# Weights cast by the GpSimd queue in four quarters, w and u read to all partitions, one PSUM pool and a new written order, in a kernel of linear attention and a squared-ReLU MLP

## The chip, the cores and the metric

One NeuronCore of a Trainium2 chip. The metric is the device time of one execution in microseconds (us); lower is better. The kernel before takes 176.31 us, the median of three runs (175.8, 176.31, 177.17).

Engines are named as the profile names them: PE (TensorE matmuls, with its weight loads PEld), DVE (VectorE), ACT (ScalarE), POOL (GpSimd), SP (SyncE, which here only issues DMAs). A queue name with q (SPq, ACTq, POOLq) is the engine as an issuer of DMAs.

## The reference

Two parts, one after the other. First a linear attention with a decaying state, for 4 batches, 8 heads, 768 time steps and head width 48:

```python
for t in range(S):
    cur = einsum('bhd,bhe->bhde', u * k[t], v[t])
    y[t] = einsum('bhd,bhde->bhe', r[t], state + cur)
    state = w * state + einsum('bhd,bhe->bhde', k[t], v[t])
```

Its result, laid out as 3072 tokens x 384, goes through an MLP: `h = max(x @ w_in, 0)` with w_in 384 x 2048, and `out = (h * h) @ w_out` with w_out 2048 x 384. All tensors are float32; the kernel works in bf16 with float32 sums.

## The kernel before, in words

The time axis is cut into 6 chunks of 128 steps; with 4 batches that makes 24 chunk-items, numbered i = 4 * chunk + batch. A chunk-item's attention is done in closed form by matmuls, and its 128 rows of output are then 128 tokens of the MLP. Tokens are grouped: chunk-items 0 and 1 are groups 1-item wide (g = 0, 1), and from there two items make a group (g = 2 is items 2 and 3, g = 3 is 4 and 5, up to g = 12).

The order of the work is written out by hand in the text `ORDER` (lines 20 to 107) and nothing reorders it: each word is one step, `name.arguments:engine/buffers`, and every engine does its own steps in the order of the text, waiting by semaphores for data and for free buffers. The steps, with their lines:

- `ld.r.i`, `ld.k.i`, `ld.v.i` (L320, on SP): load one item of r, k or v, 128 x 384 float32, in runs of 48 numbers. Each of the three has 7 buffers.
- `w`, `u` (L274, L277), `shw`, `shu` (L283, L286): w and u come as four rows into partitions 0, 32, 64 and 96, and a DVE stream shuffle copies them to all partitions. `logw`, `Wk`, `Wt` (L289 to L301, on ACT) make decay factors of w; those for the first four items are in PSUM banks.
- `kh`, `rh` (L336, L339): k and r times decay factors, in bf16, into a buffer `rk`. `T` (L363, PE) transposes `rk` for items 0 to 8 and 11, and `Tc` copies it out of PSUM; for the other 14 items `XB` (L369) does the same as a transposing DMA on SP.
- `A` (L376, PE): the 128 x 128 scores of 8 heads; `Bm` (L384, DVE): the causal mask; `vb`: v in bf16; `Y` (L392, L394, PE): output, with the state of the chunk before; `U` (L403, PE), `ts`, `S` (L421, L424): the new state, for chunk c+1 of the same batch, so `S.i` is needed by `Y.(i+4)`.
- `P0`, `P1`, `du`, `dv` (L342 to L354): the diagonal term with u; `xs` (L411, DVE) adds it to `Y`. `X` (L429, PE) with `xTc`, or `xX` (L436, a transposing DMA), gives the transposed tokens.
- `F1.g.s` (L445, PE, 8 per two-item group, 4 per one-item group): one bank of x @ w_in, which covers 512 columns of the bank; `re` (L453 on ACT, L455 on DVE) the ReLU; `sq` the square, in form 0 on ACT (L460), form 1 on DVE from the bank and the ReLU (L462), form 2 on DVE from the ReLU alone (L464). `F2.i.q` (L472, PE): a quarter of the sum of item i over w_out. `os`, `out` (L484, L487): copy out of PSUM and store.
- `Z.n.b` (L481): n matmuls that compute nothing that is used.

The weights: w_in (W1) is in eight pieces of 256 columns. Seven of them are `lW` (L324): float32 loads on SP's queue into staging buffers, in the midst of the loads of r, k and v, and `cW` casts them to bf16 (six on ACT, one on POOL). The eighth, `W.0.2`, and the four quarters of w_out (W2), `W.1.0` to `W.1.3` (L333), are DMAs on POOL's queue that cast on the way. For three of the four quarters of w_out each partition takes pairs of neighbouring rows, 3072 bytes in one run.

PSUM's eight banks are divided: 4 for attention, 2 for `F1`, 2 for `F2`.

Of the kernel before, what the change touches and what calls it, by code (L numbers as in the profile page):

```python
# [18 lines left out]
POOLS = dict(ldr=7, ldk=7, ldv=7, ws=0, wsa=4, rk=7, P0=5, dv=5, vb=8, rkT=7, bank=4, bankH=2, bankO=2, Bm=6, xs=5, xT1=2, xT2=3, xT4=1, hr=6, hq=30, os=4, ts=2)  # L19
ORDER = """  # L20
ld.r.1:S/0 w:A ld.k.1:S/0 u:S Z.48.5:P tab:A ld.k.0:S/1 ld.k.2:S/2 shw:D ld.r.0:S/1 logw:A ld.r.2:S/2 Wt:A/0 P0.1:D/0
Wk:A/1 lW.0.6:S/0 kh.1:D/0 ld.v.1:S/0 rh.1:D shu:D ld.k.3:S/3 T.1:P/0 kh.0:D/1 Z.16.5:P P1.1:G Tc.1:A/0 kh.2:D/2
rh.0:D ld.v.3:S/1 WtS:A rh.2:D P0.2:G/1 A.1:P/1/2 WkS:A T.0:P/3 lW.0.1:S/1 Z.16.5:P P1.2:D ld.r.3:S/3 Tc.0:A/1
du.1:D/0 P0.0:D/2 cW.0.6:A ld.v.0:S/2 A.0:P/0/3 dv.1:G Bm.1.1:D/0 Z.6.5:P du.2:D/1 T.2:P/2 P1.0:G Bm.1.0:D/1
ld.v.2:S/3 Z.22.5:P Tc.2:A/2 Bm.0.0:D/2 Bm.0.1:D/3 lW.0.0:S/2 vb.1:A/0 lW.0.5:S/3 kh.3:D/3 Y.1:P/1 cW.0.1:A lW.0.7:S/0
A.2:P/0/2 xs.1:D/0 Z.4.5:P P0.3:G/3 vb.3:A/1 du.0:D/2 lW.0.4:S/1 X.1:P/3 Z.8.5:P rh.3:D wc:S xTc.1:A/0 Bm.2.0:D/4
vb.0:A/2 T.3:P/1 ld.k.4:S/4 dv.0:D Y.0:P/3 Z.13.5:P Tc.3:A/3 vb.2:G/3 Bm.2.1:D/5 P1.3:G xs.0:D/1 A.3:P/0/2 X.0:P/1
cW.0.0:A U.0:P/3 dv.2:G Bm.3.0:D/1 Z.6.7:P xTc.0:A/1 du.3:D/3 lW.0.3:S/2 F1.1.0:P/0 Bm.3.1:D/0 ld.r.4:S/4 F1.0.0:P/1
re.1.0:D/0 cW.0.7:G Y.2:P/0 Y.3:P/1 re.0.0:A/1 ld.k.5:S/5 xs.2:D/2 cW.0.5:A W.1.0:G dv.3:D F1.1.3:P/0 cW.0.4:A W.0.2:G
X.2:P/2 F1.0.3:P/1 re.1.3:D/2 ld.r.5:S/5 xTc.2:A/0 W.1.1:G U.2:P/0 xs.3:D/3 F1.0.2:P/0 re.0.3:A/3 sq.1.3:D2/0 WLcol:A  # L30
X.3:P/2 F1.1.2:P/1 re.0.2:D/4 xTc.3:A WLm:G U.3:P/1 F1.2.1:P/0 re.1.2:A/5 W.1.2:G sq.0.3:A0/1 F1.2.5:P/1 re.2.1:D/2
W.1.3:G sq.0.0:A0/2 U.1:P/2 S0.2:D re.2.5:A/3 F1.2.4:P/0 sq.0.2:D2/3 cW.0.3:A S0.0:D F1.2.7:P/1 re.2.4:D/1 sq.1.0:A0/4
F2.0.0:P/1 sq.2.5:D2/5 re.2.7:A/4 S0.3:D F1.0.1:P/0 F1.2.3:P/1 re.0.1:D/0 F2.1.0:P/0 S0.1:D re.2.3:A/3 F1.1.1:P/0
sq.1.2:D2/6 sq.0.1:D2/7 ld.k.7:S/6 F1.2.0:P/1 re.1.1:A/5 F2.0.1:P re.2.0:A/0 sq.1.1:D2/8 F1.2.2:P/0 sq.2.4:A0/9
sq.2.0:D1/10 F2.1.1:P kh.4:D/4 F1.2.6:P/1 ld.v.5:S/4 rh.4:D P0.4:D/4 F2.1.2:P ld.r.7:S/6 re.2.2:D/5 P1.4:G F2.0.2:P
re.2.6:D/1 sq.2.2:A0/11 F2.1.3:P ld.v.4:S/5 kh.5:G/5 sq.2.1:A0/12 sq.2.6:D1/13 F2.0.3:P os.1:A/0 du.4:D/4 ld.k.6:S/0
T.4:P/0 sq.2.3:A0/14 rh.5:D F2.2.0:P/0 os.0:A/1 P0.5:D/0 Tc.4:A/4 ld.r.6:S/0 T.5:P/3 P1.5:D F2.2.1:P kh.7:D/6 Tc.5:A/5
ld.v.7:S/6 A.4:P/1/2 du.5:D/0 F2.3.0:P/1 Bm.4.0:D/3 ld.k.9:S/2 A.5:P/0/3 vb.4:A/4 dv.4:G Bm.4.1:D/2 F2.3.1:P vb.5:A/5
ld.r.9:S/2 Bm.5.1:D/4 dv.5:G sq.2.7:A0/15 Y.4:P/1 Bm.5.0:D/5 F2.3.2:P rh.7:G ld.k.8:S/1 xs.4:D/4 U.4:P/2 Y.5:P/3
F2.2.2:P P0.6:G/1 ld.v.6:S/0 xs.5:D/0 X.4:P/0 ts.4:D/0 X.5:P/1 T.7:P/3 xTc.4:A/1 kh.6:D/1 ld.k.15:S/3 F2.2.3:P xTc.5:A  # L40
rh.6:D vb.7:A/6 U.5:P/2 P1.6:D F1.3.0:P/0 Tc.7:A/6 ld.k.10:S/4 ts.5:D/1 F1.3.1:P/1 kh.9:D/2 re.3.0:A/0 ld.v.9:S/2
T.6:P/0 P0.7:D/2 os.2:A/2 A.7:P/1/2 S.5:D re.3.1:A/5 ld.r.8:S/1 F2.3.3:P du.6:D/2 P1.7:G Tc.6:A/0 Bm.7.1:D/0
F1.3.3:P/0 sq.3.0:A0/16 rh.9:G ld.r.10:S/3 os.3:D/3 F1.3.4:P/1 re.3.3:A/2 Bm.7.0:D/1 A.6:P/3/0 P0.9:G/3 du.7:D/1
re.3.4:A/1 XB.9:S/1 F1.3.5:P/0 Bm.6.1:D/3 sq.3.1:A0/17 dv.7:G F1.3.6:P/1 Bm.6.0:D/2 re.3.5:A/3 F2.5.0:P/0 dv.6:G
vb.6:A/7 ld.k.12:S/5 sq.3.3:A0/18 Y.7:P/2 out.3:S kh.10:D/3 re.3.6:A/4 Y.6:P/1 ld.v.8:S/3 S.4:G xs.7:D/1 F1.3.2:P/0
sq.3.5:A0/19 xs.6:D/2 F1.3.7:P/1 ld.v.11:S/1 kh.8:D/0 re.3.2:A/0 kh.15:D/4 U.6:P/0 X.6:P/3 sq.3.2:A0/20 X.7:P/2 rh.8:D
F2.4.0:P/1 ld.r.12:S/4 re.3.7:A/5 rh.10:D F2.5.1:P xTc.6:A/2 sq.3.4:D2/21 P1.9:D xTc.7:A U.7:P/1 T.8:P/3 vb.9:A/2
out.0:S P0.8:D/4 F1.4.0:P/0 ts.6:D/1 ld.k.11:S/0 Tc.8:A/2 P1.8:G ts.7:D/0 F1.4.4:P/1 ld.r.13:S/5 du.9:D/3 re.4.0:A/2
F2.5.2:P kh.12:G/5 re.4.4:A/3 F1.4.6:P/0 ld.r.11:S/0 sq.3.6:A0/23 sq.3.7:D2/22 vb.8:G/3 du.8:D/4 A.9:P/2/0
sq.4.4:A0/24 A.8:P/1/3 S.6:G re.4.6:A/0 F2.5.3:P ld.v.10:S/5 Bm.8.1:D/4 F1.4.3:P/1 dv.8:G Bm.8.0:D/5 os.5:A/3  # L50
ld.k.13:S/6 F1.4.5:P/0 Bm.9.1:D/1 re.4.3:A/1 dv.9:G Y.8:P/3 Bm.9.0:D/0 re.4.5:A/5 XB.10:S/3 F2.4.1:P P0.12:G/0
xs.8:D/3 sq.4.0:A0/25 Y.9:P/1 vb.11:A/1 kh.11:G/1 F1.4.1:P/1 xs.9:D/4 ld.v.13:S/4 X.8:P/0 F1.4.2:P/0 re.4.1:D/4
xTc.8:A/0 ld.r.15:S/6 F2.4.2:P rh.11:D sq.4.1:A0/26 P1.12:D X.9:P/2 vb.10:A/0 F1.4.7:P/1 P0.10:D/1 ld.k.20:S/2 xTc.9:A
sq.4.5:D2/27 F2.7.0:P/0 P0.11:D/2 re.4.7:A/3 ld.v.12:S/6 U.8:P/3 P1.10:D sq.4.3:A0/28 F2.4.3:P kh.13:D/6 re.4.2:A/2
F1.5.2:P/1 du.10:D/0 out.1:S os.4:A/1 rh.13:G sq.4.2:A0/29 ts.8:D/1 A.10:P/1/0 ld.k.17:S/1 F2.6.0:P/1 re.5.2:A/4
P1.11:G ld.k.14:S/5 F1.5.7:P/0 rh.12:G F1.5.1:P/1 du.11:D/1 ld.k.16:S/4 re.5.7:A/5 T.11:P/2 rh.15:D re.5.1:A/1
F1.5.0:P/0 dv.10:G Bm.10.1:D/3 Tc.11:A/4 ld.v.14:S/0 F1.5.5:P/1 vb.13:D/4 re.5.0:A/2 Bm.10.0:D/2 dv.11:G U.11:P/3
A.11:P/0/2 XB.13:S/5 sq.4.7:A0/2 F2.7.1:P S.7:D re.5.5:A/3 Bm.11.1:D/4 P0.15:G/3 Y.10:P/1 sq.5.2:A0/4 F2.6.1:P
XB.12:S/6 du.12:D/2 sq.5.5:A0/7 Bm.11.0:D/5 U.9:P/2 F1.5.6:P/0 kh.17:D/0 F2.6.2:P ld.r.14:S/2 ts.9:D/0 re.5.6:A/4
Y.11:P/0 sq.5.0:D2/8 sq.5.1:A0/6 out.2:S S.9:G xs.10:D/0 F1.5.3:P/1 sq.4.6:A0/3 ld.r.16:S/1 xs.11:D/2 F1.5.4:P/0  # L60
re.5.3:D/3 S.8:G X.10:P/2 U.10:P/1 XB.15:S/0 F2.7.2:P xTc.10:A/1 P1.15:D vb.14:A/5 F2.7.3:P ts.10:D/0 dv.12:G
ts.11:D/1 ld.r.17:S/3 X.11:P/0 F2.6.3:P os.7:A/0 kh.16:D/1 xTc.11:A kh.14:D/2 A.13:P/2/1 re.5.4:A/2 ld.k.18:S/0
A.12:P/3/0 F1.6.2:P/1 sq.5.3:A0/0 sq.5.4:D2/1 S.10:D os.6:A/2 F1.6.3:P/0 re.6.2:A/1 rh.14:D ld.v.18:S/3 F2.9.0:P/0
re.6.3:A/0 rh.16:D F1.6.6:P/1 sq.5.6:A0/10 sq.5.7:D2/12 XB.14:S/2 P0.13:D/4 F2.9.1:P Bm.13.0:D/1 P1.13:G F1.6.1:P/0
Bm.13.1:D/0 XB.16:S/1 F2.8.0:P/1 P0.14:G/1 Bm.12.1:D/3 re.6.1:A/2 F2.8.1:P Bm.12.0:D/2 sq.6.3:A0/11 P1.14:G
ld.r.18:S/0 sq.6.1:A0/14 A.15:P/2/1 F1.6.4:P/0 vb.12:A/7 out.6:S Bm.15.0:D/5 P0.17:G/2 re.6.6:A/3 ld.v.17:S/2 U.13:P/0
Y.12:P/3 du.13:D/4 re.6.4:A/5 F2.8.2:P rh.17:G xs.12:D/1 ld.v.15:S/5 F1.6.0:P/1 Bm.15.1:D/4 A.14:P/2/3 du.14:D/3
re.6.0:A/4 xX.12:S/2 U.12:P/1 dv.13:D F2.8.3:P sq.6.2:A0/9 kh.18:D/3 F1.6.5:P/0 Bm.14.0:D/3 XB.17:S/3 F1.6.7:P/1
S.11:D re.6.5:A/0 ts.13:D/0 F2.9.2:P os.8:A/2 out.7:S P0.18:D/0 sq.6.0:A0/5 Y.13:P/2 ts.12:D/1 ld.k.21:S/3
sq.6.6:A0/13 F2.9.3:P P1.18:G xs.13:D/3 sq.6.5:A0/15 ld.v.16:S/1 F2.10.0:P/1 Bm.14.1:D/2 dv.14:G X.13:P/0 du.15:D/0  # L70
F2.10.1:P ld.r.20:S/4 P0.16:G/4 re.6.7:D/2 xTc.13:A Y.14:P/1 vb.15:A/6 F1.7.5:P/0 kh.20:G/6 xs.14:D/4 ld.k.22:S/6
os.9:A/0 F1.7.6:P/1 S.12:D A.16:P/2/3 xX.14:S/0 re.7.6:A/1 P1.17:G A.17:P/0/1 F2.11.0:P/0 sq.6.7:A0/16 Bm.17.1:D/1
sq.6.4:A0/17 S.13:G F1.7.1:P/1 ld.v.20:S/6 Bm.16.1:D/0 re.7.5:A/4 F2.11.1:P ld.k.19:S/5 Bm.17.0:D/2 dv.15:G Y.15:P/1
re.7.1:D/3 ld.r.19:S/6 F1.7.0:P/0 xs.15:D/0 rh.20:G F1.7.3:P/1 re.7.0:A/0 ld.r.23:S/5 P1.16:D U.15:P/3 sq.7.1:A0/20
F2.10.2:P du.16:D/1 re.7.3:A/2 U.14:P/0 xX.15:S F1.7.2:P/0 P0.20:D/1 vb.16:A/3 dv.16:G Bm.16.0:D/3 sq.7.3:A0/18
F1.7.4:P/1 out.5:S re.7.2:A/5 rh.18:D F2.11.2:P vb.18:A/1 out.8:S sq.7.6:D2/21 re.7.4:A/3 F2.10.3:P sq.7.5:D2/19
ld.r.21:S/2 kh.19:D/5 vb.17:A/2 F1.7.7:P/0 ld.k.23:S/1 sq.7.4:A0/22 rh.19:D Y.16:P/1 kh.22:D/4 re.7.7:A/2 Y.17:P/2
# [41 lines left out]
def kernel(  # L119
# [32 lines left out]

    w_in_t = moe_w_in.rearrange("(c p) f -> p c f", p=128)
    w_out_t = moe_w_out.rearrange("(q f p) o -> q p f o", f=4, p=128)
    w_out_p = moe_w_out.rearrange("(q e p j) o -> q p e j o", e=2, p=128, j=2)


    plain = {int(t.split(":")[0].split(".")[2]) // 2 for t in ORDER.split() if t.startswith("W.0.")}
# [378 lines left out]
```

## Time and profile before

The page is of one execution, whose span from the first to the last instruction is 175.6 us; the page gives no other time of it. The runs' median is 176.31 us, so 0.7 us above the span.

| | |
|---|---|
| runs | 175.8, 176.31, 177.17 us |
| span of the profiled execution | 175.6 us |
| busy: PE, DVE, ACT, POOL | 165.1, 140.6, 109.4, 69.2 us |
| first `F1` starts | 20.50 us |
| PE's last matmul ends | 172.0 us |
| granted PE clock | 1.00 throughout |
| loads of r, k, v: issue to landing, median | 4.0, 4.1, 3.8 us |
| cast DMAs of w_out: issue to landing, least, median, most | 7.4, 10.2, 11.9 us |

How to read it: a line of groups gives line, engine, operation, what it writes and reads, its count, then busy us and mean ns of one. A row of a window gives the window, its length, then each engine's busy us with the number of instructions, the PE clock, the share of the 16 DMA engines that was busy (over 1 where queues overlap) and GB/s. A row of a DMA queue gives packets, MB and the share of the 16 engines' time. "x12" is a count of instructions.

### The profile page before, as it was taken

To read this page: it belongs to the slowest core of one execution; us is meant where nothing else is said; L and a number is where in the kernel's file an instruction comes from. 1 tells how busy PE (TensorE), PEld (TensorE's weight loads), DVE (VectorE), ACT (ScalarE), POOL (GpSimd) and SP (SyncE) were. 2 spreads that over 40 slices of the span, in tenths; PEclk is the share of its full clock that TensorE was granted. 3 is DMA by queue.
4 is the path that set the end of the run, shared out by engine and by line. 5 is a ranking of instruction groups with operands and counts; after the bars stand their busy time and mean duration, and the time that the engine had idled before them with its cause. 6 is when DMAs were issued, how large, how long until landed. Compare 5 with 4: busy or idle time off the path is not lost.

```text
span 175.6 us, 4601 instructions
## 1 busy us (share of the span) xinstructions
PE 165.1 (94%) x1813; PEld 127.0 (72%) x1813; DVE 140.6 (80%) x278; ACT 109.4 (62%) x203; POOL 69.2 (39%) x84
## 2 busy tenths in 40 slices
PE   4888797899999999999999999999999999999991
PEld 4767695666778778777767787777778677787760
DVE  4699877499899998999989899899988667853620
ACT  2479498249399987886668669669478132164401
POOL 4073582035358394926282960600960302000000
PEclk9999999999999999999999999999999999999999
DMA  5999999989899999999999979989971422110041
GB/s 105 218 217 236 315 231 187 192 166 220 163 210 106 246 207 134 232 159 242 170 162 214 212 142 223 155 203 191 199 157 26 157 90 62 33 45 0 4 169 55
DMA packets 102277, 28.36 MB, mean 161 GB/s; under 512 B 94824, under 2 KB 102256, under 8 KB 102256
## 3 DMA queue, kind: packets, MB, share of 16 engines
q1 hardware_dynamic: 100360, 26.10, 75.4%
q0 software_dynamic: 1744, 1.77, 6.1%
q8 instruction: 14, 0.23, 0.6%
q10 hardware_dynamic: 152, 0.20, 0.3%
q14 instruction: 7, 0.06, 0.1%
HBM read 20.46 MB, written 4.72 MB: 143 GB/s over the span
## 4 chain that ended last, share of the span: by engine, by line
PE 80%; DMA 10%; SPq 4%; POOL 1%; issue 1%; ACT 0%; POOLq 0%
PE bank L472 36%; PE bank L445 33%; DMA wsa<-in_moe_w_in_dram 6%; DMA W<-in_moe_w_in_dram 5%; SPq L320 4%; PE bank L376 3%; PE bank L394 2%; PE bank L392 2%; PE bank L403 2%; PE bank L363 2%; PE bank L429 1%; POOL W L262 0%; SPq L324 0%; POOL W L333 0%; ACT os L260 0%
## 5 line engine op out<-in xcount | busy, mean ns | idle before, releaser
L445 PE MATMUL bank<-xT,W 128*128 128x256 bf16 (+1 forms) x624 | 74.4, 264 | 1.6 <-ACT W L260 0.9
L472 PE MATMUL bank<-W,hq 128*128 128x384 bf16 x384 | 73.6, 326 | 1.0 <-DMA W<-in_moe_w_out_dram 1.0
L453 ACT ACTIVATE hr<-bank 128x512 bf16<-128x512 f32 x71 | 42.0, 597 | 38.9 <-PE bank L445 36.3
L445 PEld LDWEIGHTS <-W 128*128 128x128 bf16 x624 | 55.3, 98 | 12.3 <-ACT W L260 1.2
L472 PEld LDWEIGHTS <-hq 128*128 128x128 bf16 x384 | 35.6, 98 | 19.0 <-issue 1.2
L460 ACT ACTIVATE hq<-hr 128x512 bf16<-128x512 bf16 x57 | 34.7, 629 | 2.5 <-DVE hr L455 2.4
L384 DVE TENSOR_TENSOR Bm<-bank,maskJT 128x512 bf16<-128x512 f32 x48 | 31.4, 683 | 3.0 <-PE bank L376 3.0
L346 POOL TENSOR_TENSOR P<-P,ub 128x384 f32<-128x384 f32 x14 | 15.2, 1086 | 35.5 <-DVE P L342 29.8
L455 DVE TENSOR_SCALAR hr<-bank 128x512 bf16<-128x512 f32 x25 | 17.1, 689 | 11.9 <-PE bank L445 8.3
L354 POOL TENSOR_TENSOR dv<-ldv,du 128x384 f32<-128x384 f32 x19 | 16.6, 886 | 23.7 <-DVE du L349 21.6
L464 DVE TENSOR_TENSOR hq<-hr 128x512 bf16<-128x512 bf16 x35 | 15.0, 457 | 1.7 <-ACT hr L453 1.7
L411 DVE TENSOR_TENSOR xs<-bank,dv 128x384 bf16<-128x384 f32 x24 | 13.2, 553 | 2.8 <-PE bank L394 2.2
L260 ACT COPY os<-bank 128x384 f32<-128x384 f32 x18 | 8.6, 477 | 8.1 <-PE bank L472 8.1
L481 PE MATMUL bank<-identity 128*128 128x128 bf16 x139 | 11.0, 242 | 2.3 <-POOL identity masks.py:199 2.3
L349 DVE TENSOR_REDUCE du<-P 128x8 f32<-128x384 f32 x24 | 12.9, 544 | 0.2 <-POOL P L346 0.2
L342 POOL TENSOR_TENSOR P<-ldr,ldk 128x384 f32<-128x384 f32 x11 | 11.3, 1024 | 2.4 <-DMA ldr<-in_r_dram 2.4
L260 ACT COPY rkT<-bank 128x1024 bf16<-128x1024 bf16 x10 | 10.1, 1015 | 2.8 <-PE bank L363 2.7
L481 PEld LDWEIGHTS <-identity 128*128 128x128 bf16 x139 | 9.7, 111 | 2.5 <-POOL identity masks.py:199 2.3
L424 POOL TENSOR_TENSOR S0W<-ts,WLm 128x384 bf16<-128x384 f32 x7 | 7.4, 1060 | 10.0 <-PE bank L472 6.7
L394 PE MATMUL bank<-vb,Bm 128*128 128x48 bf16 x192 | 10.8, 183 | 0.4 <-ACT vb L260 0.3
L394 PEld LDWEIGHTS <-Bm 128*128 128x128 bf16 x192 | 9.5, 96 | 1.4 <-issue 0.6
L260 ACT CAST vb<-ldv 128x384 bf16<-128x384 f32 x19 | 9.6, 512 | 0.0
(61 smaller groups left out, 163.8 us busy)
## 6 DMA issues: line engine op xcount, KB each, us to landing
ldr<-in_r_dram SPq DMA_DIRECT2D x24, 192.0 KB, 4.0
ldk<-in_k_dram SPq DMA_DIRECT2D x24, 192.0 KB, 4.1
ldv<-in_v_dram SPq DMA_DIRECT2D x24, 192.0 KB, 3.8
out_dram<-os SPq DMA_DIRECT2D x23, 192.0 KB, 2.1
wsa<-in_moe_w_in_dram SPq DMA_DIRECT2D x7, 384.0 KB, 4.8
W<-in_moe_w_out_dram POOLq DMA_DIRECT2D x4, 384.0 KB, 10.2
rkT<-rk SPq DMA_TRANSPOSE x14, 4.2
W<-in_moe_w_in_dram POOLq DMA_DIRECT2D x1, 192.0 KB, 8.1
```

The lines of the kernel that those rows point to most:

```text
L260: e.copy(o, a)
L346: e.tensor_mul(t, t, ub)
L354: e.tensor_mul(dvb[slot[f"dv{i}"]], loaded("v", i), t)
L384: e.tensor_mul(Bmb[slot[f"Bm{i}{h}"]], heads(bank(f"bA{i}{h}"), 128), mask_b)
L394: e.matmul(y[:, hc, D * h : D * (h + 1)], m[h][:, hc, :], vb[:, 2 * hc + h, :], start=(c == 0), stop=True, skip_group_check=True,)
L445: e.matmul(hp[:, fi, :], W1[f // 2][:, c, 128 * (f % 2) : 128 * (f % 2 + 1)], xt[:, c, :], start=(c == 0), stop=(c == CCH - 1), skip_group ...
L453: e.activation(hr, hp, AF.Relu)
L455: e.tensor_scalar_max(hr, hp, 0.0)
L460: e.activation(hq, hr, AF.Square)
L464: e.tensor_mul(hq, hr, hr)
L472: e.matmul(bank(f"bO{i}", "bO")[:, 0:d_model], hqb[slot[f"hq{g},{f // m}"]][:, at : at + L], W2[q][:, f % 4, :], start=(f == 0), stop=(f = ...
L481: e.matmul(banks[b][:, 0:128], identity, identity, start=True, stop=True, skip_group_check=True)
```

## The change

- w_in comes in four quarters of 512 columns, `W.0.0` to `W.0.3`, all as casting DMAs on POOL's queue. `lW`, `cW` and their staging buffers are gone. w_out keeps its four casting DMAs, all now in single rows (1536 bytes in one run).
- `w` and `u` are each read to all 128 partitions by one DMA (the row is read 128 times); the shuffles and the two clearing memsets are gone.
- All 8 PSUM banks are one pool, and each step names its bank. `F2` may take its quarters in any order.
- A new ORDER. The eight `W` steps stand on POOL between attention steps, in the order W.0.0, W.0.1, W.1.0, W.0.2, W.0.3, W.1.3, W.1.1, W.1.2. Steps have also changed their engine:

| steps | before | after |
|---|---|---|
| POOL: P0, P1, S, dv | 11, 14, 7, 19 | 14, 19, 14, 21 |
| POOL: kh, rh, vb, W, cW | 5, 6, 3, 5, 1 | 12, 15, 7, 8, 0 |
| DVE: P0, P1, S, dv, kh, rh | 13, 10, 9, 5, 19, 18 | 10, 5, 2, 3, 12, 9 |
| DVE: re, sq form 1, sq form 2, vb, xTc | 25, 4, 35, 2, 0 | 33, 22, 19, 5, 3 |
| ACT: re, sq, vb, xTc, cW | 71, 57, 19, 14, 6 | 63, 55, 12, 12, 0 |
| stores issued by SP, by ACT | 23, 1 | 14, 10 |
| PE: matmuls in Z | 139 | 166 |

The transposes by PE are of items 0 to 9 in the new order, and XB does items 10 to 23.

```diff
-POOLS = dict(..., ws=0, wsa=4, ..., bank=4, bankH=2, bankO=2, ...)
+POOLS = dict(..., bank=8, ...)
...
-    W1 = [const.tile([128, CCH, 256], BF16, name=f"W1_{s}") for s in range(FCH // 2)]
+    W1 = [const.tile([128, CCH, 512], BF16, name=f"W1_{s}") for s in range(FCH // 4)]
...
         def w(e):
-            e.dma_start(out=quarter_rows(wrow), in_=row4(w))
+            e.dma_start(out=wb.rearrange("p a b -> p (a b)"), in_=row(w))
...
         def W(e, a, s):
-            e.dma_start(out=rows2(W2[s], s) if a else W1[s], in_=weights(a, s))
+            e.dma_start(out=(W1, W2)[a][s], in_=w_out_t[s] if a else w_in_t[:, :, 512 * s : 512 * (s + 1)])
...
-                    start=(f == 0), stop=(f == FCH - 1), skip_group_check=True,
+                    start=(f == 4 * q and len(done) == 1), stop=(f == 4 * q + 3 and len(done) == 4),
```

The new order, in the words that the prediction speaks of (POOL's start; PE around T.4; SP around the first XB; PE's end):

```
P1.0 W.0.0 P1.1 dv.1 W.0.1 P1.2 P0.3 P1.3 W.1.0 dv.0 dv.2 dv.3 W.0.2 W.0.3 WLm kh.4 rh.4 kh.5 W.1.3 P0.5 W.1.1 kh.6 rh.6 P1.6 W.1.2
...
F1.2.0 T.4 F2.0.0 F2.1.0 T.5 F1.1.2 F1.0.2 F1.2.4 F1.2.5 F1.1.3
...
ld.v.10 ld.r.12 out.2 ld.r.14 XB.11 XB.12 XB.10 XB.15 ld.k.20
...
F2.22.0 F1.11.2 F2.21.0 F2.21.2 F2.20.1 F2.21.1 F2.21.3 F2.20.3 F2.20.2
```

## Prediction

> **What bounds the kernel now.** I read the page first (busy shares and the 40 slices), then the chain of waits, then windows of 20 us, then the DMA queues by window, last SP's timeline.
>
> ```profile
> PE 165.1 (94%) x1813; PEld 127.0 (72%) x1813; DVE 140.6 (80%) x278; ACT 109.4 (62%) x203; POOL 69.2 (39%) x84
> DMA  5999999989899999999999979989971422110041
> q1 hardware_dynamic: 100360, 26.10, 75.4%
> q0 software_dynamic: 1744, 1.77, 6.1%
> ```
>
> PE is busy 94% of the span, but the 16 DMA engines are full as well, from the second slice to about 105 us and with few gaps to 135 us. The chain of waits says from when PE is the bound:
>
> ```profile
> 23.53 8.06 DMA W<-in_moe_w_in_dram
> 31.63 1.50 PE bank L445 x18
> ...
> 48.58 1.31 PE bank L445 x12
> ...
> 172.00 0.48 ACT os L260
> ```
>
> Up to 31.63 us the end waits for the last piece of w_in; from there to 172.0 it is PE alone. I price PE's steps by this chain (F1 and F2 0.65, T 0.45, Y 0.40, A 0.33, X and U 0.17) and call "left" what PE has still to do at a step when everything useful (152.4 us) is summed from the end of the order. It fits: 123.3 left at F1.3.0, which the chain starts at 48.58, gives 171.9. So a step that cannot start before t holds PE's end at t + left, in either order.
>
> ```profile
> 40.00:60.00 20.00, 20.00 (x248) 15.32 (x247) 19.08 (x38) 16.69 (x32) 9.73 (x11) 1.00 1.02 183
> 60.00:80.00 20.00, 20.00 (x233) 15.68 (x231) 18.88 (x35) 16.71 (x32) 14.51 (x16) 1.00 1.11 194
> 80.00:100.00 20.00, 20.00 (x226) 14.72 (x223) 18.46 (x35) 13.43 (x28) 11.03 (x12) 1.00 1.13 197
> ```
>
> In these windows PE never idles, and neither does DMA (share above 1). At 183 GB/s a load of 192 KB takes the 16 engines 1.07 us.
>
> ```profile
> q0 software_dynamic: 727, 0.62, 99.5%
> q1 hardware_dynamic: 444, 0.08, 19.0%
> ```
>
> ```profile
> q0 software_dynamic: 653, 0.63, 93.8%
> q1 hardware_dynamic: 649, 0.12, 28.2%
> ```
>
> These are the queues in 26 to 30 and 30 to 34 us. While POOL's casting DMAs run, SP's queue gets 0.20 MB in 8 us, one load's worth: the cast traffic pushes the loads of r, k and v aside. It moves 1.25 MB (as written) in 7.7 us of full engines, 2.4 us for a quarter of 0.39 MB (0.15 to 0.18 MB in windows of 1 us: 2.2 to 2.6).
>
> ```profile
> 75.18 3.81 SPq L369 DMA_TRANSPOSE rkT<-rk  x2
> ...
> 109.16 4.52 SPq L369 DMA_TRANSPOSE rkT<-rk  x2
> ```
>
> Two XB take SP 3.81 us with the engines full: 1.9 each; an xX, with 3/8 of the elements, 0.7.
>
> **A tally of DMA work, tried on the kernel before.** Start 1.9 (first bytes in the first slice), loads 1.07, stores 0.6 and float32 pieces of w_in 1.2 (0.39 MB at the 319 GB/s of 18 to 22 us), cast quarters 2.4. All weights: 7 x 1.2 + 1.2 + 4 x 2.4 = 19.2. Up to XB.12: 1.9 + 19.2 + 49 loads 52.4 + 3 stores 1.8 + 4 XB 7.6 = 82.9. Seen: its issue at 77.1 plus 3.2 to 5.3 to land, so 81.4; the tally is 1.5 late. Up to XB.18: 67 loads, 8 stores, 10 XB, 3 xX give 118.7; seen 115.6, 3.1 late. A.12 with 88.5 left is wanted at 83.5 and A.18 with 56.3 left at 115.7: slack 2.1 and 0.1. The kernel before stands on two limits at once, PE and the arrival of data.
>
> **The change, part by part.**
>
> DMA bytes of the weights: 8 quarters x 2.4 = 19.2, the same. The single rows of w_out and the longer runs of w_in may make it 2.2 or 2.6 each, -1.6 to +1.6; I take 0, since these rows hold runs of both kinds.
>
> w and u to 128 partitions: two times 192 KB at 319 GB/s, +1.2 of DMA ahead of the loads. No row shows 128 reads of one row; bounds are 0 (the four-row form is 6 KB) and 2 x 1.07. wb now waits for a DMA like a load (4.0 from the issue at 1.37, 5.4; ends 4.46 as for four rows and 6.9), where the shuffle ended at 5.06: +0.3 (-0.6 to +1.8). Two shuffles (0.58 each) leave DVE.
>
> The start: logw, Wt, Wk (0.52, 0.58, 0.57) from 5.4 give 7.05; kh.1, rh.0, kh.0 at 0.47 give T.0 at 8.5. Z.86 before it ends near 8.3 (48 took 4.55, the rest at 0.056), so it costs nothing unless rh and kh come early. Tc.0 ends 9.95, A.0 follows 0.7 later than the first A before (9.35). POOL: P1.0 9.5 to 10.5, then W.0.0; landing takes 7.4 when alone, 17.9. F1.1.0 starts near 18 and not 20.5, with the same 4.1 of PE's work behind it: 2.5 us won there. W.0.1 waits on POOL behind dv.1 (so on du.1) and lands at 21.3; W.0.2 and W.0.3 behind dv.3 land at 28.5 and 29.9. By left, F1.1.2 holds PE's end at 28.5 + 139.6 = 168.1, F1.1.3 at 166.9.
>
> The casting DMAs of this trace took 7.4 to 11.9 us to land, which is what I use. The Trainium skill, "DMA: Bandwidth & Descriptors", section "Anatomy of one DMA — SWDGE (gpsimd) path", fits 2.0 us plus bytes over 436 GB/s, an estimate of 3.8 us for the 786 KB that a quarter reads; by it W.0.0 would land at 14.3, and the end would be the same, since the steps that decide below do not wait for it. The five issues on POOL took 0.70 to 0.89 with DVE busy 71% of 20 to 28 us. A rule of the skill speaks against the change: "SBUF — State Buffer", "Summary: rules for kernel authors", would issue such a DMA elsewhere, because DVE's fast modes starve GpSimd's making of descriptors; by it each of the eight issues could grow by a DVE instruction, and no row here shows that.
>
> What is late next is T.5. PE must do it before any F1 with W.0.2, and it needs k.5 and r.5, loads 15 and 16. By then: 1.9 + 1.2 + 16 x 1.07 + five cast quarters 12.0 = 32.2, since the casts pass the loads; kh.5 on POOL is done by then, rh.5 is 0.3 more. PE's end is held at 32.5 + 140.1 = 172.6: the 2.5 us are gone. Without the 12.0 ahead it would be 160.6; with W.0.3 behind it, 170.2. W.1.3, W.1.1, W.1.2 are queued on POOL behind kh.5, P0.5 and P1.6 and land 7.4 after about 32.1, 33.2 and 37: F2.0.3 (left 132.3), F2.0.1 (131.0) and F2.0.2 (126.2) give 171.8, 171.6 and 170.6.
>
> The middle: the new order asks for data earlier against PE's progress. A.10 comes with 93.5 left, and its XB behind 50 loads, 2 stores, 2 XB: 1.9 + 1.2 + 19.2 + 53.5 + 1.2 + 5.7 = 82.7, less 1.5 as above, 81.2. With 0.3 to start, PE's end is 81.5 + 93.5 = 175.0. A.18 has 47.6 left behind all 72 loads, 11 stores, 13 XB, one xX: 131.3, less 3.7 (the lateness carried on), 127.6; 127.9 + 47.6 = 175.5. Holds are a maximum, no sum: 175.5.
>
> Engines (means of the groups): POOL gains 3 P0, 5 P1, 7 S, 2 dv, 7 kh, 9 rh, 4 vb, 3 W and loses a cast and a memset: +37, to 106. DVE -8, ACT -16 (6 casts, 8 ReLUs, 7 vb) and 9 issues of stores at 0.5 to 1.0. PE +0.2 (an X) and 27 Z ahead of F1. DVE and ACT gain slack but do not end the path, since PE is full; so 0. One pool of banks: PE has no wait for a bank from 32 to 172, so no gain; a late reader of a shared bank may stop an F1: 0 to +2, I take 0.
>
> The tail: F1.11.2 stands two steps before F2.21.2, so PE waits for a ReLU (0.60) and a square (0.46) with 0.65 of F2.21.0 for cover: +0.4 (0 to 1.5). Before, the last 40 matmuls ran 6.51 without a gap. After PE the copy and the store take the 3.6 of now.
>
> Sum: 175.5 + 0.4 + 3.6 = 179.5 against the span of 175.6, +3.9. The median stands 0.7 above that span: 180.2.
>
> **Rivals.**
> - Faster: loads are not what bounds. For: the first F1 and the last quarter of w_in come earlier, ACT and DVE have less to do. Then F1.1.2 decides: 168.1 + 0.4 + 3.6 + 0.7 = 172.8. It needs k.5 and r.5 by 28 and XB.10 by 74. Against: the queue that got 0.20 MB in 8 us, and DMA full to 105.
> - No change: T.5 decides alone, 172.6 + 4.7 = 177.3. It needs XB.10 below 78.8 and XB.18 below 124.7; the tally would have to be 2.4 to 2.9 more wrong than on the kernel before.
> - POOL becomes the bound: 43 steps from rh.12 (about 75, load 50) to rh.18, 41 us at 0.96. XB.18 waits for rh.18. If POOL idles a quarter of that time for DVE (P1 idled 29.8 in 6 waits, dv 21.6 in 5), rh.18 ends at 130, XB.18 lands 4.2 later, PE ends at 134.5 + 47.6 = 182.1: 186.8. It decides once idling passes 15%. Against: with data there POOL runs its steps back to back (14.51 of 20 us in 60 to 80).
>
> **How the numbers follow.** The forecast 0.47, faster 0.16, no change 0.19, POOL 0.18. The forecast's own range is 177.5 to 183 (weights 1.6, w and u 1.0, tail 1.1). The whole range reaches down to 174 and up to 185. About 1% is what a measurement of this kernel tells from no change: below 174.5 counts as faster (0.16), above 178.1 as slower (0.62), between lie the no-change case and the forecast's lower edge (0.22).
>
> **What would show it.** Right: first F1 near 18; PE idle before T.5 near 32 with a load behind it; idle before A.10 near 81 and A.18 near 128 by an XB; DMA share near 1 to 105; a gap of 0.4 before F2.21.2. Wrong: PE full from 28 on, or idle waits that end with POOL or with a bank's reader.

## The result, and the profile after

The changed kernel takes 179.63 us, the median of 10 runs (178.1 to 182.74); the kernel before took 176.92 us in 10 runs beside them (175.8 to 178.04). The ratio is 1.0136, with a 95% interval of 1.0094 to 1.0177: slower by 1.4%, some 2.4 us. The forecast was 180.2 us, slower, 3.9 above the 176.31 that it started from. The direction and the range came out, and most of the reasons for them did not.

Ratios here leave out runs more than 1.5% above the fastest of their kernel, medians do not, and the profiled execution of the changed kernel is itself such a run (181.42 us, a span of 179.7), so it is read for the order of events and not for tenths.

The page of the changed kernel, to be read against the first fence of the prediction:

```profile
PE 168.0 (94%) x1843; PEld 131.0 (73%) x1843; DVE 143.1 (80%) x256; ACT 96.4 (54%) x178; POOL 107.5 (60%) x122
...
DMA  4999999979999999789949988998544033001122
...
q1 hardware_dynamic: 95984, 21.67, 60.0%
q0 software_dynamic: 3712, 3.15, 11.8%
q10 hardware_dynamic: 1584, 2.16, 3.6%
```

PE is as full as before (94% of a longer span), ACT has lost 13 us, POOL has grown from 69.2 to 107.5 us as forecast (106), but DVE has not shrunk: 143.1 us and not 132.6. The DMA row stays at 7 to 9 up to the 27th slice (121 us), but for one 4; before it did so up to the 30th (132 us); q10 is ACT's queue, which now carries w's 128 reads and ten stores.

The first 24 us in windows of 4 us, of the changed kernel and then of the kernel before (columns as before: PE, PEld, DVE, ACT, POOL, then PE clock, DMA share, GB/s):

```profile
12.00:16.00 4.00, 2.37 (x45) 1.89 (x42) 3.50 (x7) 1.92 (x3) 3.27 (x4) 1.00 1.01 147
16.00:20.00 4.00, 2.02 (x33) 1.74 (x32) 2.23 (x5) 2.04 (x3) 2.04 (x3) 1.00 1.27 224
20.00:24.00 4.00, 3.96 (x50) 3.56 (x50) 2.99 (x6) 1.28 (x5) 3.98 (x6) 0.57 1.05 170
```

```profile
12.00:16.00 4.00, 3.38 (x60) 2.82 (x58) 4.00 (x8) 2.57 (x5) 1.59 (x3) 1.00 0.99 224
16.00:20.00 4.00, 3.41 (x60) 2.72 (x56) 3.81 (x8) 2.53 (x5) 2.84 (x4) 1.00 1.01 281
20.00:24.00 4.00, 3.50 (x69) 3.34 (x70) 3.09 (x7) 2.77 (x5) 2.51 (x4) 1.00 1.12 301
```

Between 12 and 20 us PE does 4.39 us of work where it did 6.79, and DVE 5.73 where it did 7.81, with the DMA engines as busy as ever. So both wait for data, and not for an engine. The wait itself, in the timeline of DVE and of PE:

```profile
17.77 0.56 DVE L303 TENSOR_TENSOR rk<-ldr,bank 128x384 bf16<-128x384 f32 x1 [1.93 <-DMA ldr<-in_r_dram]
```

```profile
18.39 0.40 PE L327 MATMUL bank<-identity,rk 128*128 128x128 bf16 x4 [0.93 <-DVE rk L303]
...
20.05 1.76 PE L448 MATMUL bank<-identity 128*128 128x128 bf16 x15 [1.09 <-DVE Bm L348]
...
23.66 0.55 PE L409 MATMUL bank<-xT,W 128*128 128x128 bf16 x7
```

`rh.3` waits 1.93 us for the load of r of item 3; `xs.1` stands behind it on DVE, `T.3` on PE, and the first `F1` (L409) starts at 23.66. Its weights were not the cause: `W.0.0` was issued at 10.72 and landed 5.7 us later, at 16.4. Before, the first `F1` started at 20.50, and there it did wait for its weights:

```profile
20.50 1.51 PE L445 MATMUL bank<-xT,W 128*128 128x128 bf16 x24 [0.88 <-ACT W L260]
```

Part of the delay belongs to this one execution. The 15 fillers at 20.05 (`Z.15`, which first wait 1.09 us until `Bm.0.1` has read their bank) took 1.76 us, with the granted clock at 0.57. The kernel with items 4 to 9 in long runs (below) has the same front; there the same fillers took 1.00 us at a clock of 1.00, and the first `F1` started at 22.73. The clock alone does not make the kernel slower, though: its runs with a mean clock of 0.996 to 1.00 took 178.1 to 179.71 us, and one 182.74, against 175.8 to 178.04 before.

From the first `F1` on the two kernels have the same 148.3 us left on PE (the prediction's 152.4 less 4.1). Before: 20.50 + 148.3 = 168.8, PE's end 172.0, so 3.2 lost behind it. After: 23.66 + 148.3 = 172.0, PE's end 176.1, so 4.1 lost. Of the 4.1 us between the two profiled executions 3.2 are lost ahead of the first `F1` and 0.9 behind it. The largest idle time behind it is again a load, r of item 6, as the chain of waits and then PE's timeline show:

```profile
26.29 11.19 DMA ldr<-in_r_dram
...
38.88 0.55 DVE S0W L382
```

```profile
39.48 0.81 PE L438 MATMUL bank<-W,hq 128*128 128x384 bf16 x4 [1.14 <-DVE S0W L382]
```

That load took 11.19 us from issue to landing, `P0.6` on DVE waited for it, and `S0.0` stood behind `P0.6`. PE's `F2.2.0` takes the bank that `S0.0` has to read first.

Where the holds of the forecast lay, PE was full (windows of 20 us, and the `XB` on SP's queue that should have been late):

```profile
60.00:80.00 20.00, 19.81 (x209) 15.95 (x210) 20.00 (x33) 17.57 (x34) 18.54 (x20) 1.00 0.92 184
80.00:100.00 20.00, 19.86 (x198) 13.95 (x197) 19.61 (x33) 9.08 (x19) 19.85 (x20) 1.00 0.97 202
100.00:120.00 20.00, 20.00 (x217) 16.02 (x212) 19.05 (x34) 12.76 (x26) 17.97 (x19) 1.00 0.93 186
120.00:140.00 20.00, 19.80 (x253) 14.86 (x251) 18.45 (x33) 9.50 (x20) 13.01 (x15) 1.00 0.61 144
```

```profile
73.50 7.05 SPq L333 DMA_TRANSPOSE rkT<-rk  x4
...
119.66 4.50 SPq L333 DMA_TRANSPOSE rkT<-rk  x2
```

PE idles 0.53 us in these 80 us. `XB.10`, the third of the first four, landed at 81.1 (forecast 81.2), and PE came to `A.10` at 82.0, straight from `A.12` and without idle time. `XB.18` landed at 126.1 (forecast 127.6), 2.3 us before PE came to `A.18`.

### The profile page after: what moved, and what is told of

It is laid out like the page before. It is cut to its first block, busy times and chain, and to the rows that moved or that the text cites. A ratio compares the mean times of both kernels' runs of the same rounds, so it can differ in the third digit from the quotient of the medians.

```text
span 179.7 us, 4642 instructions
## 1 busy us (share of the span) xinstructions
PE 168.0 (94%) x1843; PEld 131.0 (73%) x1843; DVE 143.1 (80%) x256; ACT 96.4 (54%) x178; POOL 107.5 (60%) x122
## 3 DMA queue, kind: packets, MB, share of 16 engines
HBM read 20.84 MB, written 4.72 MB: 142 GB/s over the span
## 4 chain that ended last, share of the span: by engine, by line
PE 60%; DMA 11%; SPq 9%; DVE 7%; POOL 5%; issue 3%; ACT 2%; POOLq 0%; DVEq 0%
PE bank L438 28%; PE bank L409 25%; SPq L294 8%; DMA ldr<-in_r_dram 6%; DMA ldk<-in_k_dram 5%; DVE Bm L348 2%; PE bank L340 2%; PE bank L358 2%; PE bank L367 2%; ACT hr L417 1%; PE bank L356 1%; POOL P L306 1%; POOL P L310 1%; POOL rk L303 1%; DVE hr L419 1%
## 5 line engine op out<-in xcount | busy, mean ns | idle before, releaser
L438 PE MATMUL bank<-W,hq 128*128 128x384 bf16 x384 | 69.6, 326 | 1.3 <-DVE S0W L382 1.1
L409 PE MATMUL bank<-xT,W 128*128 128x256 bf16 (+1 forms) x624 | 69.7, 264 | 0.2 <-ACT hq L424 0.2
L409 PEld LDWEIGHTS <-W 128*128 128x128 bf16 x624 | 56.1, 98 | 7.8 <-DVE xT L245 0.4
L417 ACT ACTIVATE hr<-bank 128x512 bf16<-128x512 f32 x63 | 35.7, 595 | 22.3 <-PE bank L409 22.0
L310 POOL TENSOR_TENSOR P<-P,ub 128x384 f32<-128x384 f32 x19 | 20.3, 1069 | 13.4 <-DVE P L306 13.2
L419 DVE TENSOR_SCALAR hr<-bank 128x512 bf16<-128x512 f32 x33 | 22.4, 683 | 7.3 <-PE bank L409 7.2
L303 POOL TENSOR_TENSOR rk<-ldr,Wt 128x384 bf16<-128x384 f32 x15 | 15.5, 1036 | 5.8 <-DMA ldr<-in_r_dram 5.8
L306 POOL TENSOR_TENSOR P<-ldr,ldk 128x384 f32<-128x384 f32 x14 | 15.0, 1070 | 3.5 <-DMA ldr<-in_r_dram 3.5
L388 POOL TENSOR_TENSOR S0W<-ts,WLm 128x384 bf16<-128x384 f32 x14 | 14.9, 1065 | 2.2 <-PE bank L358 2.1
L300 POOL TENSOR_TENSOR rk<-ldk,Wkhat 128x384 bf16<-128x384 f32 x12 | 13.5, 1133 | 2.4 <-DMA ldk<-in_k_dram 2.3
L426 DVE TENSOR_TENSOR hq<-bank,hr 128x512 bf16<-128x512 f32 x22 | 14.8, 681 | 0.1
```

The source lines that it names most:

```text
L303: e.tensor_mul(rk[slot[f"rk{i}"]][:, 0, :, 0:D], loaded("r", i), early("WtP") if i < EARLY else Wt2)
L306: e.tensor_mul(P0b[slot[f"P{i}"]], loaded("r", i), loaded("k", i))
L310: e.tensor_mul(t, t, ub)
L409: e.matmul(hp[:, fi, :], W1[f // 4][:, c, 128 * (f % 4) : 128 * (f % 4 + 1)], xt[:, c, :], start=(c == 0), stop=(c == CCH - 1), skip_group ...
L417: e.activation(hr, hp, AF.Relu)
L419: e.tensor_scalar_max(hr, hp, 0.0)
```

## The experiments

Theory at the outset, from these lines: the front decides, that is, the loads of items 0 to 3 come late and everything that follows is moved back. Rival, the forecast's own: the tally of DMA work in the middle decides (`XB.10`, `XB.18`). The first experiments ask which loads matter, by making some of them cheap.

**Loads of some items in long runs.** Edit, with a condition that differs:

```diff
+            if i >= 10:   # or 4 <= i < 10, or i < 4
+                e.dma_start(out=loaded(x, i).rearrange("p h d -> p (h d)"), in_=flat[x][i])
```

`flat` is the same tensor cut into 128 rows of 1536 bytes, so these items get other numbers than they should; only the time of the load is read.

Items 10 to 23:

> The changed kernel, but the loads of r, k and v for items 10 to 23 (42 of 72) read the same bytes in runs of 1536 instead of 192, so other numbers come in and the output is not the reference's; a load then costs the DMA engines 0.6 instead of 1.07 us, 20 us less in all, from about 57 us on. Theory on record (data under the new order holds A.10 and A.18): the hold goes, PE's end falls from 176 to the front's own limit of about 172.6, so 3 us less than the changed kernel, about 176.5. Rival (the front: the first F1 at 23.7 and PE's waits up to 42 us make all of the loss): nothing before 50 us changes, so within 0.7 us of the changed kernel, about 179.5.

Measured: 178.62 us, ratio to before 1.0114 (1.0061 to 1.0167). The windows show that the work did go:

```profile
60.00:80.00 20.00, 20.00 (x198) 15.77 (x196) 20.00 (x32) 18.09 (x34) 19.04 (x20) 1.00 0.55 140
80.00:100.00 20.00, 19.00 (x185) 13.36 (x186) 18.51 (x33) 8.36 (x17) 19.30 (x20) 1.00 0.78 203
```

The DMA share in 60 to 80 us fell from 0.92 to 0.55 and the time did not follow (1.0136 before the edit, intervals overlap). The tally of the middle does not decide.

Items 4 to 9:

> The changed kernel with the wide loads (same bytes, other numbers, output not the reference's) for items 4 to 9 alone: 18 loads, 8.5 us less DMA work between about 18 and 55 us. Theory on record: everything behind them in SP's queue, XB.10 and XB.18 too, comes 8 us earlier, so again about 3 us less, 176.5. Rival (front): the first F1 stays at 23.7 since its loads are of items 0 to 3; only PE's waits between 37 and 42 us go (1.5 us), about 178.

Measured: 179.93 us, 1.0176 (1.0123 to 1.0228). Nothing won.

Items 0 to 3:

> The changed kernel with the wide loads (same bytes, other numbers, output not the reference's) for items 0 to 3 alone: 12 loads, 5.6 us less DMA work in the first 20 us. Rival (front): r.3 lands 4 to 5 us earlier, the first F1 starts near 19.5 and the time falls by 3 to 4, to about 176. Theory on record: the front gains as much, and XB.10 and XB.18 also come 5 us earlier, so it gives the same number and is told apart by the other two kernels only; if the time falls by less than 2 although the first F1 is early, the front's start is not what decides.

Measured: 175.59 us, 0.9931 (0.9905 to 0.9956), 3.6 us below the changed kernel (1.0136 less 0.9931, of 177). The first `F1` starts at 19.52. The front decides; what made it late was not yet told by this.

**The cast alone, in the old order.** All of w_in by POOL's casting queue in the kernel before:

```diff
-lW.0.6:S/0 ... cW.0.6:A ...
+W.0.6:G ...
```

> The kernel before with one part of the change: all eight pieces of w_in come as casting DMAs on POOL's queue at the places where SP's loads of them stood, and the casts on ACT and POOL and the staging go. Everything else, the order too, is the old one. Theory on record: the bytes cost DMA the same and casts pass the loads of r, k, v, so the loads of items 1 to 3 come later (1.2 us for each piece that passes) but w_in itself earlier; PE waits for what is late: between 1 us faster and 3 us slower, 178 as the middle. Rival (front): the first F1 needs r.3 and k.3, which now stand behind casts, and comes 2 to 3 us later than 20.5: 178.5 to 180.

Measured: 177.95 us, 1.0064 (1.0035 to 1.0094): about 1.1 us of loss. The first `F1` started at 22.11.

**The place of the first F1.** `xs.1`, `X.1`, `xTc.1` and `F1.1.0` ahead of `rh.3` and `T.3`:

```diff
-rh.3:D ... T.3:P/7 Bm.2.0:D/4 ... xs.1:D/0 Bm.0.1:D/5 ... X.1:P/2 xTc.1:A/0 ... F1.1.0:P/7
+xs.1:D/0 ... X.1:P/2 xTc.1:A/0 ... Bm.2.0:D/4 Bm.0.1:D/5 F1.1.0:P/7 rh.3:D T.3:P/2
```

> The changed kernel, with xs.1, X.1, xTc.1 and F1.1.0 written ahead of rh.3 and T.3 on DVE, ACT and PE (T.3 takes bank 2 after X.1); the same steps otherwise. In the changed kernel F1.1.0 had its weights at 16.4 us and stood in PE's queue behind T.3, whose r.3 landed at 17.8; it started at 22.7 to 23.7. Theory 'queue': the order puts the first F1 behind a late load. Then F1.1.0 starts near 17.5, the steps behind T.3 move up by what F1.1.0 (0.7) and the wait for Bm.0.1 behind xs.1 (1.1) took, and the time is 177.6 to 178.2. Theory 'data': the late loads of items 0 to 3 hold whatever stands next, in any order; F1.1.0 starts early but the steps behind it do not, and the time is 179.0 to 179.7.

Measured: ratio 1.0066 (1.001 to 1.0122), median 180.18. The interval overlaps with that of the changed kernel, so by itself it does not tell the theories apart; the run with the front repaired, below, does.

**w and u as four rows again.** Their part of the change undone, and nothing else:

```diff
+shw:D ... shu:D
-                e.dma_start(out=wb.rearrange("p a b -> p (a b)"), in_=row(w))
+                e.dma_start(out=quarter_rows(wrow), in_=row4(w))
```

> The changed kernel with w and u read again as four rows each and copied to all partitions by two shuffles on DVE (their part of the change undone). Each read to 128 partitions is 0.2 MB in front of or among the first loads, some 0.6 us of full engines. Theory 'data': 1.2 us less DMA work in the first 8 us brings the loads of items 0 to 3 forward by up to 1.2, less 0.6 that the shuffle puts ahead of logw: F1.1.0 0.3 to 1.0 earlier, 178.6 to 179.3. Theory 'w and u cost nothing': 179.6, or 180.2 if the shuffle delays T.0 and nothing is won.

Measured: 176.86 us, 0.9937 (0.9903 to 0.9971). This is 3.5 us below the changed kernel (1.0136 less 0.9937, of 177), more than either theory allowed, and below the kernel before. The queues by window of 2 us show where it comes from. First 2 to 4 us, the changed kernel and then this one (packets, MB, share of the 16 engines' time; q10 is ACT's queue with w, q1 SP's with the loads):

```profile
q10 hardware_dynamic: 128, 0.18, 37.9%
q1 hardware_dynamic: 724, 0.14, 33.9%
```

```profile
q1 hardware_dynamic: 2076, 0.39, 100.6%
q10 hardware_dynamic: 8, 0.01, 2.7%
```

With the row read 128 times the loads get 724 packets in these 2 us, with four rows 2076. A load is 1024 packets, so this is 1.3 loads. The packets of w's queue take 37.9% of the engines' 2 us, 0.76 us; for another 0.56 us (share 0.72 in all) the engines are idle. In 6 to 8 us, where u is read, q1 has 1434 packets, 91 of them u's (the others come later), against 2163: 0.8 loads. By 12 us it has 8364 packets less u's 128, against 10487; some 200 of the latter are single numbers of `wc`, which SP issues at 9.80 here and at 12.76 in the changed kernel. That leaves 2.0 loads, 2.1 us at 1.07 each. SP's issues show the same as time, in the third load of all and at r of item 3:

```profile
1.95 2.57 SPq L294 DMA_DIRECT2D ldr<-in_r_dram  x1
...
11.90 0.74 SPq L294 DMA_DIRECT2D ldr<-in_r_dram  x1
```

```profile
1.94 0.82 SPq L311 DMA_DIRECT2D ldr<-in_r_dram  x1
...
8.40 1.28 SPq L311 DMA_DIRECT2D ldr<-in_r_dram  x1
```

The issue of the third load takes 2.57 us in place of 0.82, and r of item 3 is issued 3.5 us later. The casts were no different: in 12 to 14 us `W.0.0` pushes the loads aside in both kernels (q1 has 100 packets in either).

```profile
q0 software_dynamic: 164, 0.17, 78.6%
q1 hardware_dynamic: 100, 0.02, 4.6%
```

But with four rows r of item 3 has gone through by then: `rh.3` no longer waits (it follows its neighbour on DVE at 15.37) and the first `F1` starts at 20.00. w itself was not late in the changed kernel: `logw` started at 4.64 there and at 4.72 here. The 3.5 us are more than the 2.1 of loads; the rest was not parted, and the granted clock (0.57 in 20 to 24 us there, 1.00 here) may be in it.

```profile
15.37 0.54 DVE L320 TENSOR_TENSOR rk<-ldr,bank 128x384 bf16<-128x384 f32 x1
```

```profile
20.00 0.72 PE L426 MATMUL bank<-xT,W 128*128 128x128 bf16 x10
```

**Six loads through ACT's queue** (r.3, v.2, v.3, r.4, r.5, r.6), to see if the cast queue's share could be held off, alone and with the first `F1` moved:

```diff
-ld.r.3:S/3 ... ld.v.2:S/2 ... ld.v.3:S/3 ...
+ld.r.3:A/3 ... ld.v.2:A/2 ld.v.3:A/3 ...
```

> The changed kernel with six loads (r.3, v.2, v.3, r.4, r.5, r.6) issued by ACT at about the same moments in place of SP, so that they go through another queue. Theory 'share': while a casting DMA runs, SP's queue gets one packet for each of the cast queue's, and a second queue of loads gets a share of its own. Then r.3 takes 4 us in place of 5.9, r.6 about 5 in place of 11.2, the idle 1.1 of PE before S0.0 near 38 goes, and the time is 176.3 to 177.6. Theory 'bytes': the 16 engines are full and the sum of the bytes decides, whichever queue they come by; some loads gain and the others lose, and the time is 179.0 to 180.

> Both edits together: the first F1 ahead of T.3, and the six loads on ACT's queue. 'Queue' and 'share' both right: the two gains add up in part, 174.8 to 176.5, below the kernel before. Only one right: the time of that one alone. Neither: 179 to 180.

Measured: 190.36 us (1.0602, 1.0518 to 1.0687) and 189.71 us (1.0659, 1.0599 to 1.0719). Neither theory gave this time, and the runs do not test them: the loads came out in another order. Timelines of SP and of ACT in the first of the two:

```profile
13.60 6.81 SPq L294 DMA_DIRECT2D ldk<-in_k_dram  x4
```

```profile
13.80 0.39 ACTq L294 DMA_DIRECT2D ldr<-in_r_dram  x1
...
18.70 4.36 ACTq L294 DMA_DIRECT2D ldv<-in_v_dram  x2
```

With six loads gone from its list SP went straight on to four loads of k for later items, while ACT issued r of item 3 at 13.80 (SP had done so at 11.90) and v of items 2 and 3 from 18.70, behind its copies. Whether a second queue gets a share of its own beside the casts stays open.

**w and u alone, in the kernel before.** The same two DMAs put into the old order, no shuffles:

```diff
-shw:D ... shu:D
-                e.dma_start(out=quarter_rows(wrow), in_=row4(w))
+                e.dma_start(out=wb.rearrange("p a b -> p (a b)"), in_=row(w))
```

> The kernel before with this part of the change alone: w and u read to all 128 partitions by one DMA each, no shuffles. Undoing this part in the changed kernel took 3.5 us off. Theory 'reads': the two DMAs take 2.3 us from SP's loads in the first 12 us whatever the order behind them, and the lost time is passed on to the first F1: 178.8 to 180.5. Theory 'order': only the new order, whose first F1 stands behind more of the loads, is hurt; before has slack there and lands between 176 and 177.8.

Measured: 179.64 us, 1.0175 (1.0122 to 1.0228), 3.1 us. So the loss comes with this part in either order. The queues in 2 to 4 us, then SP's queue in the kernel before, then the first `F1`:

```profile
q10 hardware_dynamic: 131, 0.18, 40.3%
q1 hardware_dynamic: 800, 0.15, 37.3%
```

```profile
q1 hardware_dynamic: 2088, 0.40, 99.9%
```

```profile
23.22 0.95 PE L435 MATMUL bank<-xT,W 128*128 128x128 bf16 x14
```

800 packets of loads where the kernel before had 2088, and a first `F1` at 23.22 and not 20.50. The values of w and u are not what is late: `logw` starts at 4.49 (5.10 before) and POOL's first `P1`, which needs u, at 7.98 (8.38 before). Nor is it the clock (0.62 in 16 to 20 us of this profile): a run with a mean clock of 1.00 took 179.49 us.

**w alone as four rows:**

> The changed kernel with w alone as four rows and a shuffle; u is still read to 128 partitions, behind four loads in SP's queue. It parts the 3.5 us. If every such read costs loads its own time in equal parts: about 178.2. If the first one costs more, because no load gets through until its 128 reads are out of the way (in the first 4 us the loads got 724 packets in place of 2105, for u 1434 in place of 2163 from 6 to 8): 177.4 to 178.0.

Measured: 177.14 us, 1.0014 (0.9971 to 1.0057). Between 1.0136 and 0.9937 that gives w 1.2% (2.2 us) and u 0.8% (1.4 us). The first read may cost more, as its packets did, but the intervals leave room for equal parts, and the time is below what either theory allowed.

**The first F1 moved up, with the front repaired:**

> The changed kernel with w and u in four rows and also the first F1 ahead of T.3, as in the run before. Theory 'data': with the reads gone r.3 is there before rh.3's turn, so the place of F1.1.0 matters little: 176.5 to 177.2. Theory 'queue': F1.1.0 starts near 17 in place of 20, and 0.7 to 1.5 is won: 175.4 to 176.2.

Measured: 176.46 us, 0.9964 (0.9939 to 0.999).

> Four rows; xs.1 and X.1 moved up further, ahead of Bm.2.1, so that F1.1.0 follows its weights (near 16.3); and wc's two DMAs of single numbers behind v.2 and v.3 on SP's queue. Theory 'queue': 175.0 to 176.0, below the kernel before by 1%. Theory 'data': what stands behind T.3 sets the end, and it is 176.5 to 177.2 as without these moves.

Measured: 176.63 us, 0.9992 (0.9959 to 1.0025). Neither is below the four rows alone (0.9937), though the first `F1` starts 2.0 and 3.3 us earlier. The profiled executions of four kernels (the time of PE's end is its last group's):

| kernel | first F1 | second half of T.5 | PE's end |
|---|---|---|---|
| loads of items 0 to 3 in long runs | 19.52 | 28.99 | 170.1 |
| four rows | 20.00 | 29.17 | 171.2 |
| four rows, first F1 moved | 18.03 | 29.37 (whole) | 171.3 |
| four rows, first F1 moved further, wc later | 16.67 | 29.43 | 171.5 |

PE's end follows `T.5` and not the first `F1`. The earlier run with the first `F1` moved and w and u still read to all partitions fits this: first `F1` at 17.98, second half of `T.5` at 30.86, PE's end at 174.5. Already the second `F1` comes no earlier; with four rows, and in the last kernel of the table:

```profile
21.21 0.83 PE L426 MATMUL bank<-xT,W 128*128 128x128 bf16 x12
```

```profile
21.14 0.83 PE L427 MATMUL bank<-xT,W 128*128 128x128 bf16 x12
```

The first `F1` has changed places with `T.3`, `A.3` and the fillers, which now stand behind it. In this last kernel PE also waits at `T.5` for `rh.5`:

```profile
29.43 0.40 PE L345 MATMUL bank<-identity,rk 128*128 128x128 bf16 x4 [0.77 <-DVE rk L321]
```

```profile
27.80 1.57 DVE L321 TENSOR_TENSOR rk<-ldr,Wt 128x384 bf16<-128x384 f32 x1
```

The theory "queue" fell. The kernel with four rows is the best that was run with the reference's output: 0.63% below the kernel before (0.29 to 0.97), within what the forecast called no change.

Put together, of the kernel before:

| what | ratio | us of 177 |
|---|---|---|
| w and u read to all partitions, alone | 1.0175 | +3.1 |
| the cast of all w_in by POOL's queue, alone | 1.0064 | +1.1 |
| the whole change without w and u | 0.9937 | -1.1 |
| the whole change | 1.0136 | +2.4 |

Each ratio is against runs of the kernel before on the same chip, so differences between rows carry both intervals. If the cast costs in the new order what it costs in the old, the new order, the single pool of banks and the work moved to POOL, which were not parted, bring 2.2 us (-1.1 less 1.1); w and u take 3.1 to 3.5 and turn the sign.

## Why the prediction was right, and where it was not

**The step that failed** is "F1.1.0 starts near 18 and not 20.5, with the same 4.1 of PE's work behind it: 2.5 us won there". It was 3.2 lost, or 2.2 where the clock stayed at 1.00 (22.73). The term under it that was mis-sized is "w and u to 128 partitions: two times 192 KB at 319 GB/s, +1.2 of DMA ahead of the loads", with bounds of 0 and 2.14. It measured 2.0 loads by 12 us, 2.1 us at 1.07 each, which is the upper bound, and 3.1 to 3.5 in the time. The size by bytes left out that the engines stood partly idle while w's packets went (share 0.72). A second thing was wrong with its use: the 1.2 went into the tallies for `T.5` and the `XB`, and not into r of item 3, which has 9 loads ahead of it and `xs.1`, `T.3` and the first `F1` behind it. I asked there only for the weights.

**The steps that were to decide**, "PE's end is 81.5 + 93.5 = 175.0" and "175.5" for `A.18`, fell: the tally placed `XB.10` well (81.2, seen 81.1), but PE came to `A.10` later than that and to `A.18` later still, so it idled at neither, and 20 us of DMA work less in that stretch changed nothing that can be measured. That 175.5 + 0.4 = 175.9 stands beside a seen 176.1 is an accident: 3.2 us more ahead of the first `F1` and 0.9 more behind it, in place of a single hold. A tally fitted on the kernel before, and then used to a tenth on another order, carries no hold of its own.

**T.5.** "PE's end is held at 32.5 + 140.1 = 172.6": `T.5` did start at 32.43, but PE came to it without idle time, after `rh.5` had run directly behind its neighbour on DVE. It does hold once the front is earlier, and the forecast had named it as "what is late next". With w and u read to all partitions it was the load, as forecast (`rh.5` waits 1.31 us for r of item 5 in the run with the first `F1` moved); with four rows `rh.5` followed its neighbour on DVE without such a wait.

**One pool of banks.** "A late reader of a shared bank may stop an F1: 0 to +2, I take 0": PE did wait for such readers, 1.09 us at 20.05 (`Z.15` for `Bm.0.1`) and 1.14 us at 39.48 (`F2.2.0` for `S0.0`), which the prediction had named as a sign of being wrong. Both readers stood behind late loads on DVE, and with four rows the second wait does not appear. What the single pool costs or wins by itself was not tested.

**Right**: wb was there for logw at 4.64 (forecast 5.4, bound 6.9), `T.0` started at 8.71 (8.5), right behind `Z.86`, POOL's busy time and the 3.6 us behind PE's end. The eight issues of casts took 0.77 to 0.94 us each.

**Wrong in passing**: the gap of 0.4 before `F2.21.2` did not come:

```profile
171.54 4.59 PE bank L438 x28
```

28 matmuls in 4.59 us are 164 ns each, without a gap. DVE was to lose 8 us and gained 2.5 (below). And "the median stands 0.7 above that span" mixed two runs: every run lists its span, and the time is 1.7 above it each time, so the profiled execution of before, with its span of 175.6, was one of about 177.3 us, and the sum came out 1.0 too low.

**The rivals.** "Faster: loads are not what bounds" failed on its own condition, early loads; with the four rows the same change is 0.6% faster. "POOL becomes the bound" (186.8) did not happen: POOL ran 19.85 of 20 us in 80 to 100, and PE was full there. The rival that was missing is the one that decided: the added reads themselves, at the head of the queue that bounds, dearer than their bytes.

## What to carry to other kernels

When a kernel's start is a queue of loads, price what a change puts at the head of that queue by the first thing that everything waits for, and count every load behind it; two reads that save two instructions of 0.58 us on an engine with slack can cost 3 us. Price such a read by packets and by what the engines fail to do meanwhile, since bytes at the best rate are only the lower bound. And a "hold" at a step stands only until the next one: moving the first `F1` up by 3.3 us won nothing, because the second came no earlier (21.14 against 21.21).

## What the runs showed of the hardware

**One row read 128 times.** w's 128 packets of 1536 bytes took 102 ns each on average; in the kernel with items 0 to 3 in long runs, the loads' packets of that size from different places took 68 ns (457 of them, in 4 to 6 us). And SP's loads, issued at the same 0.81 us, moved 55 packets up to 3 us, against 1021 with four rows. Why the loads wait for w's packets was not tried. ACT issued w at the same 0.81, so the order of issue does not tell.

**DVE slows beside POOL.** Groups of DVE by form, after, then before:

```profile
L428 DVE TENSOR_TENSOR hq<-hr 128x512 bf16<-128x512 bf16 x19 | 11.3, 608 | 2.1 <-ACT hr L417 2.1
L385 DVE TENSOR_TENSOR ts<-bank,S0W 128x384 f32<-128x384 f32 x16 | 8.6, 545 | 0.7 <-PE bank L367 0.7
...
L318 DVE TENSOR_TENSOR dv<-ldv,du 128x384 f32<-128x384 f32 x3 | 3.2, 1072 | 0.0
```

```profile
L464 DVE TENSOR_TENSOR hq<-hr 128x512 bf16<-128x512 bf16 x35 | 15.0, 457 | 1.7 <-ACT hr L453 1.7
...
L421 DVE TENSOR_TENSOR ts<-bank,S0W 128x384 f32<-128x384 f32 x16 | 8.5, 548 | 0.2 <-PE bank L403 0.2
...
L354 DVE TENSOR_TENSOR dv<-ldv,du 128x384 f32<-128x384 f32 x5 | 2.7, 548 | 0.0
```

`dv` and the square in form 2 read both operands from SBUF: 1072 and 608 ns with POOL at 107.5 us, 548 and 457 with POOL at 69.2. `ts`, with one operand in PSUM, stays at 545 and 548. With four rows, and POOL at 108.4 us, `dv` took 1038, the square 546 and `ts` 546. In the kernel with the first `F1` moved further `rh.5` took 1.57 us and not 0.55 at 27.80, and PE waited for it.
The Trainium skill, "SBUF — State Buffer", section "SBUF: two separate sides", says that a DVE instruction with two SBUF inputs and a GpSimd instruction that reads SBUF lock each other out for a whole instruction; these rows agree, and the +37 us on POOL should have been charged to DVE. The same page's "Summary: rules for kernel authors", cited in the prediction against casts on POOL's queue, did not show: the issues took 0.77 to 0.94 us (0.70 to 0.89 before), and the casts of w_out landed sooner (median 7.4 us, 10.2 before). The rule speaks of DVE in its fast modes, and no row tells in which mode DVE ran.

**The clock of PE.** In the changed kernel's profile PE was busy 2.02 of 4 us in 16 to 20, and the granted clock fell to 0.57 in 20 to 24. In the kernel with items 4 to 9 in long runs it was busy 1.85 of 4, and the clock stayed at 1.00. So a stretch that is about half idle was followed by a lower clock in one execution and not in another; what decides it was not tested.
